# Masks and selector of a windowed attention built behind the branch instead of ahead of it (one Trainium2 core)

## The chip, the core and the metric

The kernel runs on one core of one Trainium2 chip. The metric is the device time of one execution in microseconds (us). Engines are named as in the profile: PE is TensorE, DVE is VectorE, ACT is ScalarE, POOL is GpSimd, SP is SyncE, which issues the transfers (DMAs). A "q" behind a name (DVEq) is the engine's sequencer, which runs register and branch instructions.

## The reference

Attention with a local window and a few global keys and a distance bias, then two gated convolution networks:

```python
scores = scale * np.matmul(q, k.transpose(0, 1, 3, 2))        # B, H, S, D = 2, 8, 768, 64
is_global = pos[None, :] < int(n_global)                      # 8
is_local = (rel >= 0) & (rel < int(n_local))                  # 96
dist = np.where(is_global & ~is_local, float(n_local), np.abs(rel))
scores = np.where(keep, scores + -slopes * dist, -1000000000.0)
a = softmax(scores)                                           # keep = is_global | is_local
x = np.matmul(a, v)                                           # to (B, S, 512)
x = (sigmoid(causal_conv5(x)) * (x @ w_val)) @ w_out
h = np.maximum(x @ w_in, 0.0)                                 # 1024 wide
out = (h * sigmoid(conv3(h))) @ w_out2
```

## The kernel before

**Tiles.** The attention runs over 12 tiles of 128 queries (2 sequences x 6). A tile sees its own 128 keys and the 128 before them (a window of 256 columns); the first tile of a sequence sees only its own. Into the first 32 columns of the block before, which no query of the window reaches, the first keys of the sequence are copied (`first_keys`), so that the global keys are in the window too.

**One tile.** `scores` makes the scores of four heads at a time on PE (L293); VectorE adds the bias and finds the extreme (L301 with the bias array `B` for a tile with two blocks; L303 to L305 with the distance array `d0` for a tile with one block); ACT takes the exponential (L307). `weights_t` transposes the result on PE (L350, against the identity `ident`) and ACT copies it back (L352); `outputs` multiplies with the values (L362). `sums`, `turn` and `spread` bring the reciprocal sums into the layout of the output with a small matmul against a constant, the selector `sel` (L340). Between these steps `fill()` takes the next piece of other work: weights come in 0.5 MB pieces (`fetch`, L108), are converted from the form in which they lie in memory (`to_f32`, L82 to L86) and prepared, and later the dense networks run.

**The constants.** `positions` makes the index arrays `rel`, `ge` and `key` from two iotas. `masks` makes from them and from the two limits (`lf`, from `li`, read from memory) the arrays `loc`, `d0`, `k0` and `d`, and from `d` the bias `B` of the eight heads, on GpSimd (L248). `selector` makes `sel` with a memset and two selects on GpSimd (L203, L206) and a copy on ACT (L210). All of these use parts of the tile `x` as scratch.

**The branch.** The kernel has two arms: a fast one for limits that fit the window, and a general one. Every engine loads the two limits from memory into registers (L704), compares them and branches (L754). An engine does this in its own order of instructions: behind whatever the program put ahead of it. `positions`, `masks`, `make_identity` and `selector` stand ahead of the branch; SP's transfers of the limits and of the first tile's keys and queries too (L699, L701). All other transfers are issued behind it.

**The order.** On PE the instructions stand as written. On the other engines a scheduler orders them by its own estimates; `first()` (L376 to L408) raises the first tiles' steps above the fills. `fast_attention` begins with transfers, then the first tile's scores, and then goes through the tiles `t`, with `START` = 6 of them in a loop of its own.

Of the kernel before, what the change touches and what calls it, by code (L numbers as in the profile page):

```python
# [12 lines left out]
AF = mybir.ActivationFunctionType  # L13
ALU = mybir.AluOpType
# [3 lines left out]
P = 128  # L18
# [8 lines left out]
WIN = 2 * P  # L27
# [8 lines left out]
BIG = NEG * 2.0 ** NH * 1.01  # L36
# [21 lines left out]
def slope(h):  # L58
    return 2.0 ** (-8.0 * (h + 1) / NH)
# [139 lines left out]
def selector(c):  # L199

    nc = c.nc
    e = c.x[0 : 2 * NH, 0:2, XP : XP + 2 * P].rearrange("r a (h d) -> r a h d", d=D)
    nc.gpsimd.memset(e, 1.0)  # L203

    for sign, base in ((1, 0), (-1, 1)):
        nc.gpsimd.affine_select(  # L206
            out=e, in_=e, compare_op=ALU.is_ge, fill=0.0, base=base, pattern=[[-8 * sign, 2], [-2 * sign, 4], [0, D]], channel_multiplier=sign
        )
    c.sel = c.const.tile([2 * NH, NPAIR, P], F32R, name="sel")
    nc.scalar.activation(c.sel.rearrange("r (a n) c -> r a (n c)", a=2), e.rearrange("r a h d -> r a (h d)"), AF.Copy)  # L210


def positions(c):

    nc = c.nc
    t = c.x[:, 2:4, XP : XP + 3 * WIN].rearrange("p a (n w) -> p a n w", w=WIN)
    c.rel, c.ge, c.loc = (t[:, 0, n] for n in range(3))
    c.key, c.k0, c.d = t[:, 1, 0, 0:P], t[:, 1, 0, P:], t[:, 1, 1]
    it, ic = t[:, 1, 1].bitcast(I32), t[:, 1, 2, 0:P].bitcast(I32)
    nc.gpsimd.iota(it, pattern=[[-1, WIN]], base=P, channel_multiplier=1)  # L220
    nc.vector.tensor_copy(c.rel, it)
    nc.vector.tensor_scalar(c.ge, c.rel, 0.0, None, ALU.is_ge)
    nc.gpsimd.iota(ic, pattern=[[1, P]], base=0, channel_multiplier=0)
    nc.vector.tensor_copy(c.key, ic)


def masks(c):


    nc = c.nc  # L230
    lf = c.const.tile([P, 2], F32, name="lf")
    nc.vector.tensor_copy(lf, c.li[:, :, 0])
    ng, nl = lf[:, 0:1], lf[:, 1:2]
    rel, loc, d, key, k0 = c.rel, c.loc, c.d, c.key, c.k0
    c.d0 = d0 = c.const.tile([P, P], F32, name="d0")
    nc.vector.scalar_tensor_tensor(loc, rel, nl, c.ge, ALU.is_lt, ALU.mult)
    nc.vector.scalar_tensor_tensor(d0, rel[:, P:], nl, loc[:, P:], ALU.subtract, ALU.mult)
    nc.vector.scalar_tensor_tensor(k0, key, ng, loc[:, P:], ALU.is_lt, ALU.max)
    nc.vector.tensor_scalar(k0, k0, -BIG, BIG, ALU.mult, ALU.add)
    nc.vector.scalar_tensor_tensor(d0, d0, nl, k0, ALU.add, ALU.add)  # L240
    nc.vector.tensor_scalar(key[:, 0:GW], key[:, 0:GW], ng, None, ALU.is_lt)
    nc.vector.tensor_scalar(d, loc, -BIG, BIG, ALU.mult, ALU.add)
    nc.vector.tensor_scalar(d[:, 0:GW], key[:, 0:GW], -BIG, BIG, ALU.mult, ALU.add)
    nc.vector.tensor_tensor(d[:, GW:], d[:, GW:], rel[:, GW:], ALU.add)
    nc.vector.tensor_scalar(d[:, 0:GW], d[:, 0:GW], nl, None, ALU.add)
    c.B = c.const.tile([P, NH, WIN], F32, name="B")
    for h in range(NH):
        nc.gpsimd.tensor_scalar(c.B[:, h, :], d, -slope(h) / QKSCALE, 1.0, ALU.mult, ALU.mult)  # L248


def fast_attention(c, ap, fill):
# [6 lines left out]
    nc, ident = c.nc, c.ident  # L258
# [4 lines left out]
    def load_kq(t):  # L263
        if t:
            kq[t] = ap.tile([P, NPAIR, 2, P], F32, tag="kq", bufs=KQBUFS, name="kq")
            nc.sync.dma_start(kq[t], c.kq[tiles[t]])
        else:
            kq[t] = c.first
# [75 lines left out]
    def weights_t(t, pr, tags="tx"):  # L344
        nw = len(blocks(t))
        pt = c.psum.tile([P, 2, 2, P], F32, tag=tags[pr % 2], name="pt")
        for z in range(2):
            w = p.pop((t, 2 * pr + z))
            for j in range(nw):
                nc.tensor.transpose(pt[:, z, j, :], w[:, j * P : (j + 1) * P], ident)  # L350
        pts[t, pr] = ap.tile([P, 2, 2, P], F32, tag="pts", bufs=PTBUFS, name="pts")
        nc.scalar.activation(pts[t, pr][:, :, :nw, :], pt[:, :, :nw, :], AF.Copy)  # L352
# [28 lines left out]

    load_kq(0)
    load_kq(1)
    fill()
    load_v(0)
    load_kq(2)
# [6 lines left out]
    for t in range(START):  # L393
        after = t + 1 < START
        if t:
            load_kq(t + 2)
        with first():
            weights_t(t, 0, "ff")
            if t:
                turn(t - 1)  # L400
            if after:
                scores(t + 1, 0)
            if t:
                spread(t - 1)
            weights_t(t, 1, "ff")
        for n in range(FILLS[t] // 2):
            fill()
        with first():  # L408
            weights_t(t, 2, "ff")
            if after:  # L410
                scores(t + 1, 1, "o")
                first_keys(t + 1)
            if t:
                scaled(t - 1)
            weights_t(t, 3, "ff")
            sums(t)
        for n in range(FILLS[t] // 2, FILLS[t]):
            fill()
        if after:
            with first():  # L420
                outputs(t)
            load_v(t + 2)
# [260 lines left out]
@with_exitstack  # L683
def attention_gated_mlps(ctx, tc, kq, v, nn, w_val, conv_w, w_out, w_in2, w_out2, out):
    nc = tc.nc
    c = Ctx()
    c.nc, c.tc, c.kq, c.v, c.out = nc, tc, kq, v, out
    c.nn = nn.bitcast(I32)
    c.w_val, c.conv_w, c.w_out, c.w_in2, c.w_out2 = (w.bitcast(I32) for w in (w_val, conv_w, w_out, w_in2, w_out2))

    c.const = ctx.enter_context(tc.tile_pool(name="const", bufs=1))
    c.big = ctx.enter_context(tc.tile_pool(name="big", bufs=BIGBUFS))
    c.wst = ctx.enter_context(tc.tile_pool(name="wst", bufs=1))
    c.sg = ctx.enter_context(tc.tile_pool(name="sg", bufs=1))
    c.x = new_x(c)

    c.first = c.x[:, 0:2, XP + 2 * P : XP + 6 * P].rearrange("p j (n t s) -> p j n t s", n=2, t=2)
    c.li = c.const.tile([P, 2, 2], I32, name="li")
    nc.sync.dma_start(c.li.rearrange("p n t -> p (n t)"), c.nn.to_broadcast([P, 4]))  # L699
    for j in range(2):  # L700
        nc.sync.dma_start(c.first[:, j], kq[0, 0, :, 2 * j : 2 * j + 2])  # L701
    positions(c)
    masks(c)
    _, (glo, ghi, llo, lhi) = nc.values_load_multi_w_load_instructions(c.nn)  # L704
    narrow = (llo >= 1) * (llo <= PREV + 1) * (glo >= 0) * (glo <= GW) * ((lhi | ghi) == 0)
    one = c.const.tile([P, 1], F32, name="one")
    nc.vector.memset(one, 0.0)
    nc.scalar.activation(one, one, AF.Exp)
    c.ident = c.const.tile([P, P], F32, name="ident")
    make_identity(nc, c.ident)  # L710
    selector(c)

    def psum_tiles(pool):
        bufs = {"s": 2, "t": 1, "x": 1, "f": 2, "o": 2}
        r = Ctx()
        r.tile = lambda shape, dt, tag, name: pool.tile(shape, dt, tag=tag, name=name, bufs=bufs[tag])
        return r

    chunks = [(b, ch) for b in range(NB) for ch in range(NCH)]

    def arm(fast):
        with ExitStack() as es:
            c.psum = psum_tiles(es.enter_context(tc.tile_pool(name="ps", bufs=1, space=PSUM)))
            c.inputs, c.written, c.taken, c.wo2 = [], 0, 0, []
            c.ready = inputs(c, chunks)

            def between():
                yield from weights(c)
                yield from dense(c, chunks)

            work = between()
            fills = iter(range(1 << 20))

            def fill():
                if next(fills) == 1:
                    load_conv_weights(c)
                next(work, None)

            with tc.tile_pool(name="at", bufs=1) as ap:
                if fast:  # L740
                    with tc.manual_schedule(engines={mybir.EngineType.PE}):
                        fast_attention(c, ap, fill)
                        for _ in work:
                            pass
                else:
                    load_conv_weights(c)
                    for b, _ in enumerate(full_attention(c, ap)):

                        while c.taken < (b + 1) * NCH:
                            next(work)  # L750
                    for _ in work:
                        pass

    with tc.If(narrow != 0) as cmp:  # L754
        arm(True)
    with cmp.Else():
        arm(False)
# [40 lines left out]
```

## Time and profile before

| | |
|---|---|
| median of 3 runs | 319.53 us (319.44 to 320.73) |
| profiled execution | 318.94 us, of which its span (first to last instruction) is 317.2 us |
| PE busy | 285.9 us, 90% of the span |
| DVE busy | 239.2 us, 75% |
| ACT busy | 208.4 us, 66% |
| POOL busy | 11.0 us, 3% |
| mean TensorE clock granted | 0.982 of 2.4 GHz |

Times in the profile count from the start of the span. Busy times leave out register, branch and transfer-issuing instructions. PE's matmuls are pipelined, so a busy PE is not PE at its peak.

### The profile page before, as it was taken

Reading aid. Unit: us, or ns where it says so; the run is one execution under the profiler, and the core shown is the slowest. Engines: PE = TensorE matmul, PEld = TensorE weight load, DVE = VectorE, ACT = ScalarE, POOL = GpSimd, SP = SyncE. Lnnn points to the kernel's source line nnn. Section 1 sums busy time; section 2 is a strip of 40 time slices with the busy share of each in tenths; the row PEclk is TensorE's granted clock in tenths of the full one; section 3 lists DMA queues with packets and bytes.
Section 4 is the critical chain, followed back from the end, with each engine's and each line's share of the span. In section 5 each row is a group of like instructions: output and inputs, shape, how many; then the busy total and the mean of one; then the engine's idle time right before and its main releaser. Section 6 shows DMA issues by size and latency. Waiting matters only on the chain.

```text
span 317.2 us, 5891 instructions
## 1 busy us (share of the span) xinstructions
PE 285.9 (90%) x2156; PEld 241.6 (76%) x2156; DVE 239.2 (75%) x660; ACT 208.4 (66%) x522; POOL 11.0 (3%) x31
## 2 busy tenths in 40 slices
PE   2169799797899999999999999999899989999993
PEld 2048556466867579999899988998899979999982
DVE  5397999989799998897765688673698379833750
ACT  2197897967596489688585786862577168615651
POOL 4400000200000000000000000000000000000000
PEclk9996999999799999999999999999999999999999
DMA  4993391257432302030210100100000001000002
GB/s 151 339 402 143 122 308 52 68 178 274 164 132 69 110 22 69 2 107 3 83 59 33 44 0 3 42 35 0 2 33 35 0 0 68 0 2 34 35 1 76
DMA packets 9494, 26.21 MB, mean 83 GB/s; under 512 B 1392, under 2 KB 1392, under 8 KB 9456
## 3 DMA queue, kind: packets, MB, share of 16 engines
q1 hardware_dynamic: 9456, 25.74, 23.0%
q8 instruction: 19, 0.31, 0.4%
q14 instruction: 19, 0.16, 0.1%
HBM read 22.59 MB, written 3.15 MB: 81 GB/s over the span
## 4 chain that ended last, share of the span: by engine, by line
PE 66%; DVE 16%; ACT 9%; DMA 5%; issue 2%; DVEq 1%; ACTq 0%; SPq 0%
PE po L74 7%; PE po L76 7%; PE ph L74 7%; PE ph L75 7%; PE po L75 7%; PE ph L76 6%; PE xp L362 5%; PE pt L350 4%; PE s L293 4%; PE pv L74 4%; PE pv L75 4%; PE pv L76 3%; ACT p L307 3%; DVE p L301 3%; DVE z L536 3%
## 5 line engine op out<-in xcount | busy, mean ns | idle before, releaser
L307 ACT ACTIVATE p<-p,st 128x256 f32<-128x256 f32 (+1 forms) x96 | 45.8, 479 | 18.3 <-DVE st L301 10.8
L74 PE MATMUL ph<-gg,Wh 128*128 128x258 f32 x192 | 55.9, 291 | 0.6 <-DVE Wl L69 0.6
L75 PE MATMUL ph<-gg,Wh 128*128 128x258 f32 x192 | 54.6, 284 | 1.6 <-DVE gg L69 1.6
L76 PE MATMUL ph<-gg,Wl 128*128 128x258 f32 x192 | 53.8, 280 | 0.0
L536 DVE SCALAR_TENSOR_TENSOR zh<-h,cw,zh 128x256 f32<-128x256 f32 x96 | 44.7, 481 | 11.0 <-ACT zh L534 9.2
L536 DVE SCALAR_TENSOR_TENSOR z<-x,cw,z 128x258 f32<-128x258 f32 x96 | 40.0, 480 | 1.7 <-ACT z L534 1.7
L350 PE MATMUL pt<-ident,p 128*128 128x128 f32 x176 | 27.6, 289 | 14.7 <-ACT p L307 10.0
L75 PEld LDWEIGHTS ph<-gg,Wh 128*128 128x128 f32 x192 | 36.4, 189 | 3.7 <-DVE gg L69 2.0
L74 PEld LDWEIGHTS ph<-gg,Wh 128*128 128x128 f32 x192 | 36.1, 188 | 3.1 <-DVE Wl L69 0.8
L74 PE MATMUL po<-wo,g 128*128 128x512 f32 x96 | 38.2, 398 | 0.0
L76 PE MATMUL po<-wo,g 128*128 128x512 f32 x96 | 37.9, 395 | 0.0
L75 PE MATMUL po<-wo,g 128*128 128x512 f32 x96 | 37.7, 393 | 0.0
L76 PEld LDWEIGHTS ph<-gg,Wl 128*128 128x128 f32 x192 | 36.6, 191 | 0.0
L350 PEld LDWEIGHTS pt<-ident,p 128*128 128x128 f32 x176 | 20.3, 145 | 20.5 <-issue 9.0
L301 DVE CUSTOM_DVE_ANT_0 p<-s,B 128x256 f32<-128x256 f32 x80 | 29.0, 418 | 2.1 <-PE s L293 2.0
L74 PE MATMUL pv<-gx,wvh 128*128 128x258 f32 x96 | 28.4, 295 | 0.8 <-DVE Wl L69 0.8
L352 ACT ACTIVATE pts<-pt 128x512 f32<-128x512 f32 (+1 forms) x48 | 24.9, 552 | 5.0 <-PE pt L350 4.9
L75 PE MATMUL pv<-gx,wvh 128*128 128x258 f32 x96 | 28.0, 291 | 0.0
L76 PE MATMUL pv<-gx,wvl 128*128 128x258 f32 x96 | 27.7, 289 | 0.0
L620 ACT ACTIVATE h<-ph 128x258 f32<-128x258 f32 x48 | 18.1, 378 | 12.2 <-PE ph L76 11.7
L293 PE MATMUL s<-kq 64*128 64x128 f32 x320 | 25.8, 296 | 0.0
L293 PEld LDWEIGHTS s<-kq 64*128 64x128 f32 x320 | 21.6, 198 | 5.0 <-issue 4.0
(99 smaller groups left out, 539.0 us busy)
## 6 DMA issues: line engine op xcount, KB each, us to landing
raw<-in_moe_w_out_dram SPq DMA_DIRECT2D x12, 512.0 KB, 4.0
kq<-in_kq_dram SPq DMA_DIRECT2D x11, 512.0 KB, 4.1
raw<-in_moe_w_in_dram SPq DMA_DIRECT2D x8, 512.0 KB, 5.5
v<-in_v_dram SPq DMA_DIRECT2D x12, 256.0 KB, 3.1
out_dram<-o SPq DMA_DIRECT2D x12, 256.0 KB, 2.0
raw<-in_moe_w_val_dram SPq DMA_DIRECT2D x4, 512.0 KB, 4.8
x<-in_kq_dram SPq DMA_DIRECT2D x2, 256.0 KB, 3.5
v<-in_v_dram SPq DMA_DIRECT2D x8, 64.0 KB, 2.5
```

Of the source, the lines that this page charges most:

```text
L74: nc.tensor.matmul(out, lh, rh, start=first, stop=False)
L75: nc.tensor.matmul(out, lh, rl, start=False, stop=False)
L76: nc.tensor.matmul(out, ll, rh, start=False, stop=last)
L293: nc.tensor.matmul(out, rows_of(t, pr, 1)[hs], rows_of(j, pr, 0)[hs], start=True, stop=True)
L301: nc.vector.tensor_tensor_reduce(w, sc, c.B[:, h, :], -QKSCALE, 3.0e38, ALU.add, ALU.min, mn)
L307: nc.scalar.activation(w[:, :nk], w[:, :nk], AF.Exp, bias=mn, scale=scale, accum_out=sm)
L350: nc.tensor.transpose(pt[:, z, j, :], w[:, j * P : (j + 1) * P], ident)
L352: nc.scalar.activation(pts[t, pr][:, :, :nw, :], pt[:, :, :nw, :], AF.Copy)
L362: nc.tensor.matmul(xp[z * D : (z + 1) * D, pr, :], vs[j][:, 2 * pr + z, :], w[:, z, n, :], start=n == 0, stop=n == len(js) - 1,)
L536: nc.vector.scalar_tensor_tensor(z, src[:, k : k + n], w[:, k : k + 1], z, ALU.mult, ALU.add)
L620: nc.scalar.activation(h[:, f % 2, :], ph[:, :HW], AF.Relu, scale=0.25)
```

## The change

`masks` is called inside the fast arm, behind the issue of the first transfers; `selector` inside the loop over the tiles, in the first pass. `positions` stays ahead of the branch, behind the identity. In `masks` the product `loc` is made in two halves of 128 columns, with `d0` and `k0`, which the first tile needs, between them in the source. The selector's copy goes from ACT to GpSimd.

```diff
@@ selector
-    nc.scalar.activation(c.sel.rearrange("r (a n) c -> r a (n c)", a=2), e.rearrange("r a h d -> r a (h d)"), AF.Copy)
+    nc.gpsimd.tensor_scalar(
+        c.sel.rearrange("r (a n) c -> r a (n c)", a=2), e.rearrange("r a h d -> r a (h d)"), 1.0, 1.0, ALU.mult, ALU.mult
+    )
@@ masks
-    nc.vector.scalar_tensor_tensor(loc, rel, nl, c.ge, ALU.is_lt, ALU.mult)
-    nc.vector.scalar_tensor_tensor(d0, rel[:, P:], nl, loc[:, P:], ALU.subtract, ALU.mult)
-    nc.vector.scalar_tensor_tensor(k0, key, ng, loc[:, P:], ALU.is_lt, ALU.max)
-    nc.vector.tensor_scalar(k0, k0, -BIG, BIG, ALU.mult, ALU.add)
-    nc.vector.scalar_tensor_tensor(d0, d0, nl, k0, ALU.add, ALU.add)
+    for z in (slice(P, WIN), slice(0, P)):
+        nc.vector.scalar_tensor_tensor(loc[:, z], rel[:, z], nl, c.ge[:, z], ALU.is_lt, ALU.mult)
+        if z.start:
+            nc.vector.scalar_tensor_tensor(d0, rel[:, z], nl, loc[:, z], ALU.subtract, ALU.mult)
+            nc.vector.scalar_tensor_tensor(k0, key, ng, loc[:, z], ALU.is_lt, ALU.max)
+            nc.vector.tensor_scalar(k0, k0, -BIG, BIG, ALU.mult, ALU.add)
+            nc.vector.scalar_tensor_tensor(d0, d0, nl, k0, ALU.add, ALU.add)
@@ fast_attention
     load_kq(1)
+    masks(c)
     fill()
...
             weights_t(t, 1, "ff")
+        if t == 0:
+            selector(c)
         for n in range(FILLS[t] // 2):
@@ attention_gated_mlps
-    positions(c)
-    masks(c)
     _, (glo, ghi, llo, lhi) = nc.values_load_multi_w_load_instructions(c.nn)
...
     make_identity(nc, c.ident)
-    selector(c)
+    positions(c)
```

Line numbers of the changed kernel are 2 to 7 higher than those of the kernel before from `masks` on.

VectorE, from the end of its work ahead of the branch to the first tile's first score operation (`x` holds the scratch arrays, `d_81` is `d0`, `p` the scores with bias). Before:

```order
L240 SCALAR_TENSOR_TENSOR d_81<-d_81,lf,x 128x128
L243 TENSOR_SCALAR x<-x 128x32
L244 TENSOR_TENSOR x<-x 128x224
L245 TENSOR_SCALAR x<-x,lf 128x32
L704 TENSOR_LOAD in_n_dram_ptr
L704 TENSOR_LOAD in_n_dram
L754 COMPARE_AND_BRANCH
L303 SCALAR_TENSOR_TENSOR p<-d_81,s_266 128x128
```

And with the change (L239 to L249 are `masks`, L307 the first score operation, L308 the reduce behind it):

```order
L223 CAST x<-x 128x256
L226 CAST x<-x 128x128
L224 TENSOR_SCALAR x<-x 128x256
L709 TENSOR_LOAD in_n_dram_ptr
L709 TENSOR_LOAD in_n_dram
L759 COMPARE_AND_BRANCH
L234 CAST lf<-li 128x2
L239 SCALAR_TENSOR_TENSOR x<-x,lf 128x128 x2
L248 TENSOR_TENSOR x<-x 128x224
L307 SCALAR_TENSOR_TENSOR p<-d_214,s_262 128x128
L249 TENSOR_SCALAR x<-x,lf 128x32
L83 TENSOR_SCALAR raw<-raw 128x512 x2
```

The register loads now stand ahead of the masks. The scheduler put both halves of L239 side by side and all of `masks` but its last instruction (L249, before: L245) ahead of the first score operation; L249 stands behind the first tile's last reduce, and two conversions of weights (L83) follow.

GpSimd, from the iotas to the bias arrays. Before:

```order
L223 IOTA x 128x128
masks.py:197 MEMSET ident 128x128
L203 MEMSET x 16x2x256
masks.py:199 AFFINE_SELECT ident<-ident 128x128
L206 AFFINE_SELECT x<-x 16x2x256 x2
L248 TENSOR_SCALAR B<-x 128x256 x8
L704 TENSOR_LOAD in_n_dram_ptr
L704 TENSOR_LOAD in_n_dram
L754 COMPARE_AND_BRANCH
L313 TENSOR_SCALAR gl<-x 128x128
```

And with the change:

```order
L225 IOTA x 128x128
L709 TENSOR_LOAD in_n_dram_ptr
L709 TENSOR_LOAD in_n_dram
L759 COMPARE_AND_BRANCH
L317 TENSOR_SCALAR gl<-x 128x128
L203 MEMSET x 16x2x256
L206 AFFINE_SELECT x<-x 16x2x256 x2
L210 TENSOR_SCALAR sel<-x 16x512
L252 TENSOR_SCALAR B<-x 128x256 x8
```

The selector's four instructions and the eight of `B` moved behind the branch, and the copy of the first keys (`gl`) ahead of them.

ACT, in the first and the second tile (128x128 is an exponential of the first tile, 128x256 of the second, `ina` converted weights). Before:

```order
L307 ACTIVATE p,st<-p,st 128x128 x4
L82 ACTIVATE ina<-raw 128x512
L307 ACTIVATE p,st<-p,st 128x256 x4
L352 ACTIVATE pts<-pt 128x2x128 x2
L307 ACTIVATE p,st<-p,st 128x256 x4
L307 ACTIVATE p,st<-p,st 128x128
```

And with the change:

```order
L311 ACTIVATE p,st<-p,st 128x128 x5
L356 ACTIVATE pts<-pt 128x2x128
L311 ACTIVATE p,st<-p,st 128x256 x2
L356 ACTIVATE pts<-pt 128x2x128
L311 ACTIVATE p,st<-p,st 128x256 x6
```

The first tile's last exponential moved ahead of the second tile's, and the conversion of weights (L82) behind them.

## Rows read from the trace of the kernel before

**Rows 1.** Busy time in two stretches: start and end, length, each engine (instructions), granted clock.

```profile
14.76:90.00 75.24, 64.43 (x501) 47.16 (x502) 69.59 (x222) 60.98 (x170) 3.49 (x6) 0.93 0.54 193
90.00:200.00 110.00, 109.23 (x904) 93.22 (x903) 91.97 (x270) 81.60 (x219) 1.23 (x4) 1.00 0.15 49
```

**Rows 2.** The chain that ended last, its first long piece: start, length, what.

```profile
0.80 3.08 DMA li<-in_n_dram
```

**Rows 3.** Line 704, the register loads: duration in ns (least/median/most), start in us.

```profile
L704 PEldq TENSOR_LOAD <-in_n_dram_ptr x1: 908/908/908, 0.9 to 0.9; - x1
L704 PEldq TENSOR_LOAD <-in_n_dram x1: 1697/1697/1697, 1.9 to 1.9; - x1
L704 SPq TENSOR_LOAD <-in_n_dram_ptr x1: 1342/1342/1342, 2.2 to 2.2; - x1
L704 SPq TENSOR_LOAD <-in_n_dram x1: 592/592/592, 3.6 to 3.6; - x1
...
L704 DVEq TENSOR_LOAD <-in_n_dram_ptr x1: 2468/2468/2468, 7.6 to 7.6; - x1
...
L704 DVEq TENSOR_LOAD <-in_n_dram x1: 2232/2232/2232, 10.1 to 10.1; - x1
```

**Rows 4.** Timeline, DVE and PE, 4 to 14 us: start, busy, what [idle before].

```profile
4.64 0.49 DVE L236 SCALAR_TENSOR_TENSOR x<-x,lf 128x256 f32<-128x256 f32 x1
...
4.94 2.08 PE L293 MATMUL s<-x 64*128 64x128 f32 x16 [4.94 <-DMA x<-in_kq_dram]
...
5.51 0.74 DVE L238 SCALAR_TENSOR_TENSOR x<-x,lf 128x128 f32<-128x128 f32 x1
...
7.11 0.34 DVE L240 SCALAR_TENSOR_TENSOR d<-d,lf,x 128x128 f32<-128x128 f32 x1
...
7.76 0.23 DVE L245 TENSOR_SCALAR x<-x,lf 128x32 f32<-128x32 f32 x1
...
13.17 0.29 DVE L303 SCALAR_TENSOR_TENSOR p<-d,s 128x128 f32<-128x128 f32 x1 [5.18 <-issue]
```

**Rows 5.** Timeline, POOL, 5 to 21 us.

```profile
5.16 0.28 POOL masks.py:199 TENSOR_SCALAR_AFFINE_SELECT ident<-ident 128x128 f32<-128x128 f32 x1
5.40 1.56 POOL L206 TENSOR_SCALAR_AFFINE_SELECT x<-x 16x512 f32<-16x512 f32 x2
8.08 3.33 POOL L248 TENSOR_SCALAR B<-x 128x256 f32<-128x256 f32 x8 [1.11 <-DVE x L245]
...
20.25 0.30 POOL L317 TENSOR_SCALAR kq<-gl 128x128 f32<-128x128 f32 x1 [5.08 <-issue]
```

**Rows 6.** Timeline, DVE and ACT, 16 to 23 us.

```profile
16.65 0.42 DVE L83 TENSOR_SCALAR raw<-raw 128x512 int32<-128x512 int32 x1
...
17.18 0.68 DVE L84 SCALAR_TENSOR_TENSOR raw<-raw 128x512 int32<-128x512 int32 x1
...
17.90 0.42 DVE L301 CUSTOM_DVE_ANT_0 p<-s,B 128x256 f32<-128x256 f32 x1
...
20.28 0.42 DVE L301 CUSTOM_DVE_ANT_0 p<-s,B 128x256 f32<-128x256 f32 x1
...
22.85 0.39 ACT L307 ACTIVATE p<-p,st 128x128 f32<-128x128 f32 x1
```

**Rows 7.** A transfer's issue (timeline, SP), and its kind: KB each, median us to landing, before 24 us.

```profile
7.79 0.37 SPq L266 DMA_DIRECT2D kq<-in_kq_dram  x1
...
kq<-in_kq_dram SPq DMA_DIRECT2D x3, 512.0 KB, 8.5
```

**Rows 8.** Busy time and granted clock from 20 to 28 us (columns as in rows 1); timeline, PE.

```profile
20.00:24.00 4.00, 1.02 (x6) 0.54 (x6) 4.00 (x19) 4.00 (x16) 0.30 (x1) 0.82 0.94 375
24.00:28.00 4.00, 4.00 (x31) 3.25 (x31) 3.38 (x13) 2.70 (x7) 0.00 (x0) 0.50 0.52 177
...
26.95 2.08 PE L293 MATMUL s<-kq 64*128 64x128 f32 x16
...
30.76 1.16 PE L293 MATMUL s<-kq 64*128 64x128 f32 x16
```

## Prediction

> **What bounds the kernel now.** I began with the page's busy times: PE works 90% of the span (the table above), so TensorE sets the end wherever it has work to do. The windows say where it has: from 90 to 200 us PE is busy 109.2 of 110.0 us, from 14.76 to 90 us 64.4 of 75.2 us [rows 1], and before 14.76 us hardly at all. What is saved there must come from the stretch before 14.76 us, and it reaches the end only if all that follows can begin earlier too.
>
> So I read the chain of waits from its beginning. Its first piece is the transfer of the two limits, 0.80 to 3.88 us [rows 2], which is what VectorE waits for before the masks. Then come VectorE's mask instructions, to 7.99 us (L245), and then nothing until 13.17 us: 5.18 us that the timeline calls issue, that is, without a wait for another engine or a transfer [rows 4]. The rows of line 704 tell what this is: every engine reads the two limits into registers for the branch, with two loads in a row, and VectorE's loads took 2.47 and 2.23 us, starting at 7.6 and 10.1 us [rows 3]. The first score operation of the first tile (L303) starts at 13.17 us [rows 4], 0.85 us after the second load's end (10.1 + 2.23 = 12.3). PE had made those scores by 7.02 us [rows 4] and stood idle. The same two loads took PE 0.91 + 1.70 = 2.61 us at the start, and SP 1.34 + 0.59 = 1.93 us from 2.2 us on [rows 3]. What differs is the hour: when its own loads are done, at 4.2 us (3.6 + 0.59), SP goes on to issue all the large transfers. Their effect on the loads is my reading of these rows, not a row of its own.
>
> **The change, step by step.**
>
> *VectorE reaches the branch earlier.* Ahead of it there stay two casts and a comparison, which need only GpSimd's two iotas; the identity's memset and select (0.28 us [rows 5]) now stand before or between these. SP begins its loads at 2.2 us; I take 2.1 us for VectorE. The limits' transfer no longer holds it there: it has landed (3.88 us) when the masks come.
>
> *The loads.* I take PE's pair, 2.61 us, because it too ran beside another engine's loads; now four engines load between 2 and 5 us. That gives 4.7 us, and with the same 0.85 us behind it the first mask instruction at 5.55 us. The ends: SP's pair, 1.93 us (0.7 earlier), and VectorE's own, 4.70 us (2.1 later). The Trainium skill (DMA: Bandwidth & Descriptors, "Latency and other measured facts") gives about 600 ns as the floor of such a load; the trace agrees in SP's second (0.59 us) and in no other; two at that floor would make the gain about 1.4 us larger.
>
> *The masks ahead of the first score.* Now they run from 4.64 us (L236) to 7.76 us (start of L245): 3.12 us [rows 4]. L245's counterpart stands behind the first tile now. Added are the cast of the limits (at most L245's 0.23 us) and the split of L236 into two halves of 128 columns (twice L240's 0.34 less 0.49: 0.2 us). So 3.5 us, and the first score at 9.05 instead of 13.17 us: **4.1 us earlier**. PE's scores are ready by then, and their keys come with transfers that don't move.
>
> How far GpSimd stretches this is the doubtful part. Today L238 took 0.74 us beside the selector's two selects (1.56 us), where L240, of the same kind and shape, took 0.34 us with GpSimd idle [rows 4, 5]. In the changed kernel the same selects, the copy of the first keys (0.30) and the selector's copy (512 columns on 16 partitions; 0.30 us at 128 and 3.33/8 = 0.42 us at 256 columns make some 0.65 us, an estimate) fall into the same stretch, so I leave today's stretching in. Without any, two such delays (L238 and L239) go: 0.7 us earlier. With every one of these 0.30 + 1.56 + 0.65 = 2.5 us added to an unstretched 2.8 us, the first score is at 10.85 us, 1.8 us later.
>
> ACT loses the selector's copy, which lay in ACT's wait for the first exponential: nothing. GpSimd's copy is needed only by the spreading matmuls behind the third tile's first scores, which start at 26.95 us [rows 8]: nothing beyond the stretching above. That lines P to WIN of the masks are made first by itself gains nothing I can price: the order below puts nearly all of the masks ahead of the first score all the same.
>
> *The eight biases B.* Today they run from 8.08 to 11.41 us [rows 5], while VectorE stands still. Now they wait for L245's counterpart, behind the eighth head of the first tile, and take 3.33 us beside a busy VectorE. They are due one by one: the next tile's first score operation (L301) came 4.73 us after the first L303 (17.90 - 13.17), and its second four 7.11 us after it (20.28 - 13.17) [rows 6]. The first tile's own share of the 4.73 us is 3.6 us (less an L83 and an L84), so B starts near 12.7 us. Up to the second four the new order adds L245 (0.23) and one L83 (0.42) and drops an L86 (as long as an L84, 0.68) and an L83 for an L84 and a small sum (some 0.2): net +0.4 us, so 16.55 instead of 20.28 us. The two L83 and two L84 on this way can each wait for a B: between nothing and 4 x 0.42 = 1.7 us. L301 itself doesn't seem to: GpSimd's copy at 20.25 us lay beside an L301 that took 0.42 us, its usual time [rows 5, 6]. I take the middle, 0.85 us: **0.4 + 0.85 us given back**, 2.9 us left. By the Trainium skill (SBUF — State Buffer, "Who interferes with whom") a VectorE instruction in a two-port mode or with two SBUF inputs and a GpSimd instruction that reads SBUF exclude each other, whichever starts first; one with a single SBUF input is free. On L301 the trace agrees; taken at its word for the rest it gives the second rival.
>
> *ACT's order.* Today the last exponential of the first tile stands behind all of the next tile's (22.85 us, 0.39 us [rows 6]) and the transposes wait for it. Now it stands ahead: **0.4 us won**, 3.3 us in all.
>
> *What carries it to the end.* PE's order is unchanged instruction for instruction. VectorE and ScalarE are reordered as far as about 100 us, but do the same work there, and from 14.76 to 90 us VectorE is busy 69.6 of 75.2 us and ScalarE 61.0 [rows 1]: all of it follows the first score, so it slides as one. The first transfers don't slide, since SP's way to them is unchanged. The 0.5 MB keys of the third tile are issued at 7.79 us and land, by the median of their kind, 8.5 us later [rows 7], near 16.5 us; PE uses them at 26.95 us now and would at 23.6: still in time. The later weight transfers wait for buffers and slide with the work.
>
> The sum: 4.1 - 0.4 - 0.85 + 0.4 = 3.3 us. The profiled execution took 318.94 us, 0.6 us under the median of 319.53 us; from the median that makes **316.2 us**. No change means within 0.5%, 1.6 us, about what a measurement of this kernel tells apart.
>
> **Rivals.**
>
> *More than that.* The loads take SP's 1.93 us (+0.7), nothing is stretched (+0.7) and B excludes nobody (+0.85): 5.5 us, 314.0 us. For it: L301 beside GpSimd kept its time. Against: L238 did not. The granted clock could add to it: 0.50 (1.2 GHz) from 24 to 28 us, after four microseconds in which PE was busy 1.02 us, made 16 score matmuls take 2.08 us where they took 1.16 us at 2.4 GHz [rows 8]. If that low stretch falls on other work the time moves by a microsecond either way. Chance 0.18.
>
> *Given back on the port.* GpSimd and VectorE exclude each other for every shared microsecond: the first score at 10.85 us (-1.8) and B's full 1.7 us (another -0.85): 0.65 us left, 318.9 us, no change. Also here: the gain is swallowed because a reordered conversion of weights comes too late for a matmul. Chance 0.16 together.
>
> *The loads block each other (slower).* PE's second load took 1.70 us while SP's first was under way; SP's second, beside nobody, 0.59 us [rows 3]. If each further engine adds such 1.1 us, four sharers make 0.59 + 4.4 = 5.0 us a load and 10 us a pair instead of 2.6: VectorE's first score comes later than today, and SP's first large transfer too: 3.3 - 7.4 = 4.1 us lost, 323.6 us. It decides from a pair of 5.9 us on. Against it: SP's first load was beside PE's second and took only 1.34 us. Chance 0.06.
>
> **How the numbers follow.** The forecast, 316.2 with 314.7 to 317.8 of its own for the bounds of load and port that don't fall together, has 0.60. Faster by over 0.5% (below 317.9) is the forecast and the first rival, 0.78; no change 0.16; slower 0.06. The range leaves out the slow rival, half of the unchanged cases and a little of the best: 313.8 to 318.4.
>
> **What would show it.** Right: VectorE's pair of loads from about 2.1 us and no longer than 2.6 us; first mask instruction near 5.6 us, first score near 9 us (8.3 to 10.9), the next tile's second four near 17.4 us, its last exponential near 20 us, and from there every stage about 3.3 us earlier. The loads are wrong if the pair takes over 4 us; the port is wrong if L238's and L239's counterparts are short, or if L83 and L84 beside B are as short as today; the carrying is wrong if the first score is early and the stage at 90 us is not. A first score later than 12 us would refute the forecast.

## The result, and the profile after

The changed kernel took **315.59 us** (median of 20 runs, 314.26 to 318.56), the kernel before 319.44 us beside it (20 runs, 317.32 to 324.29). The ratio is 0.9906, with a 95% interval of 0.9882 to 0.9930: 2.2 to 3.8 us faster, 3.0 us in the middle. The ratio is taken over the fast runs alone, so it is not the quotient of the two medians, and it is the one to go by. The forecast was 316.2 us, 3.3 us faster; its range of 313.8 to 318.4 us holds the time. The profiled execution took 314.69 us, with a span of 313.0 us where the kernel before had 317.2.

Busy times on the page of the changed kernel:

```profile
span 313.0 us, 5893 instructions
PE 283.6 (91%) x2156; PEld 239.8 (77%) x2156; DVE 240.4 (77%) x661; ACT 208.1 (66%) x521; POOL 12.0 (4%) x32
```

The work is the same but for one VectorE instruction more, one on ScalarE less and one on GpSimd more. The two stretches of [rows 1], in the changed kernel:

```profile
14.76:90.00 75.24, 62.97 (x528) 45.39 (x526) 70.81 (x216) 62.11 (x167) 4.48 (x11) 0.98 0.56 201
90.00:200.00 110.00, 108.98 (x885) 94.10 (x886) 89.95 (x263) 81.47 (x218) 1.24 (x4) 1.00 0.14 47
```

Before 90 us PE is busy 62.97 us instead of 64.43, with 27 more matmuls in the stretch and a granted clock of 0.98 instead of 0.93, and behind 90 us it is as busy as it was (108.98 and 109.23 us): the work slid forward, and PE still waits before 90 us. The loads of the two limits, now line 709 (columns as in [rows 3]):

```profile
L709 PEldq TENSOR_LOAD <-in_n_dram x1: 1647/1647/1647, 1.9 to 1.9; - x1
L709 DVEq TENSOR_LOAD <-in_n_dram_ptr x1: 1504/1504/1504, 2.0 to 2.0; - x1
...
L709 DVEq TENSOR_LOAD <-in_n_dram x1: 591/591/591, 3.6 to 3.6; - x1
```

VectorE's pair takes 1.50 + 0.59 = 2.10 us where it took 4.70 us [rows 3]. Its timeline (columns as in [rows 4]; L307 and L305 are L303 and L301 of before). Scores come in groups of four heads; the "second four" is the second group of the second tile, here the line at 16.60 us:

```profile
5.01 0.17 DVE L234 CAST lf<-li 128x2 f32<-128x2 int32 x1 [2.55 <-issue]
...
6.52 0.68 DVE L243 TENSOR_SCALAR x<-x 128x128 f32<-128x128 f32 x1
...
8.01 0.80 DVE L248 TENSOR_TENSOR x<-x 128x224 f32<-128x224 f32 x1
8.73 0.47 DVE L307 SCALAR_TENSOR_TENSOR p<-d,s 128x128 f32<-128x128 f32 x2
...
12.49 0.75 DVE L83 TENSOR_SCALAR raw<-raw 128x512 int32<-128x512 int32 x2
13.16 0.68 DVE L84 SCALAR_TENSOR_TENSOR raw<-raw 128x512 int32<-128x512 int32 x1
14.14 0.42 DVE L305 CUSTOM_DVE_ANT_0 p<-s,B 128x256 f32<-128x256 f32 x1 [0.30 <-POOL B L252]
...
16.00 0.69 DVE L84 SCALAR_TENSOR_TENSOR raw<-raw 128x512 int32<-128x512 int32 x1
16.60 0.41 DVE L305 CUSTOM_DVE_ANT_0 p<-s,B 128x256 f32<-128x256 f32 x1
```

The first score operation starts at 8.73 us instead of 13.17 [rows 4], 4.44 us earlier. The second tile's second four start at 16.60 instead of 20.28 us [rows 6], 3.68 us earlier: 0.76 us were given back on the way. `B` has 0.30 us of this by the wait shown, and some 0.2 us more: the first four L305 of the second tile start at 14.14, 14.62, 14.99 and 15.38 us, 1.24 us from first to last, where the second four take 1.03 us. GpSimd's timeline, and the instructions that write `B` (the columns of [rows 3]):

```profile
12.60 4.83 POOL L252 TENSOR_SCALAR B<-x 128x256 f32<-128x256 f32 x8 [4.03 <-DVE st L309]
```

```profile
L252 POOL TENSOR_SCALAR B<-x x8: 404/405/1512, 12.6 to 17.0; 128x256 f32<-128x256 f32 x8
```

The one of them that starts at 16.1 us, by itself:

```profile
L252 POOL TENSOR_SCALAR B<-x x1: 798/798/798, 16.1 to 16.1; 128x256 f32<-128x256 f32 x1
```

`B` takes 4.83 us instead of 3.33 [rows 5]. Two of the eight are longer than the 0.40 us of the other six. The first took 1.51 us: it lies beside two L83 and an L84. The seventh took 0.80 us: it lies beside the L84 at 16.00 us. The VectorE instructions kept their 0.42 us (L83) and 0.68 us (L84; the two L83 take 0.75 us together, as they overlap).

How far the gain reaches is seen from SyncE's first transfers of results, first before and then after the change:

```profile
164.54 2.51 SPq L637 DMA_DIRECT2D out_dram<-o  x2
```

```profile
159.68 2.50 SPq L644 DMA_DIRECT2D out_dram<-o  x2
```

Here the distance is 4.9 us, over 1 us more than at 16.6 us. The two executions differ in their granted clock as well: that of before was at 0.52 of full speed from 22.80 to 29.60 us and at 0.53 from 80.80 to 84.20 us, that of after at 0.55 from 49.10 to 52.50 us (and both in about their last microsecond). The interval from the many runs, 2.2 to 3.8 us, is what counts for the change. The clock is not what makes it: over their runs the mean granted clock was 0.984 for the changed kernel and 0.981 for the kernel before (its 85 runs beside the experiments). A difference of 0.003 over 316 us is 1.9 us at half speed, where PE's work takes 1.8 times as long [rows 8]: at most 0.9 of the 3.0 us, an estimate.

### The profile page after: what moved, and what is told of

It reads as the page before. It is cut to its first block, busy times and chain, and to the rows that moved or that the text cites. A ratio compares the mean times of both kernels' runs of the same rounds, so it can differ in the third digit from the quotient of the medians.

```text
span 313.0 us, 5893 instructions
## 1 busy us (share of the span) xinstructions
PE 283.6 (91%) x2156; PEld 239.8 (77%) x2156; DVE 240.4 (77%) x661; ACT 208.1 (66%) x521; POOL 12.0 (4%) x32
## 4 chain that ended last, share of the span: by engine, by line
PE 66%; DVE 17%; DMA 7%; ACT 5%; issue 2%; POOL 1%; DVEq 0%; POOLq 0%; ACTq 0%; SPq 0%
PE ph L74 7%; PE ph L75 7%; PE ph L76 7%; PE po L74 7%; PE po L76 7%; PE po L75 7%; DMA raw<-in_moe_w_out_dram 5%; PE xp L366 4%; PE s L297 4%; PE pv L74 3%; PE pv L75 3%; PE pv L76 3%; PE pt L354 3%; DVE p L305 3%; PE wps L178 2%
## 5 line engine op out<-in xcount | busy, mean ns | idle before, releaser
L305 DVE CUSTOM_DVE_ANT_0 p<-s,B 128x256 f32<-128x256 f32 x80 | 29.1, 418 | 0.7 <-PE s L297 0.4
L74 PE MATMUL pv<-gx,wvh 128*128 128x258 f32 x96 | 27.8, 290 | 0.3 <-DVE Wl L69 0.3
L75 PE MATMUL pv<-gx,wvh 128*128 128x258 f32 x96 | 27.3, 284 | 0.0
L366 PE MATMUL xp<-pts,v 128*64 128x128 f32 x352 | 22.5, 277 | 4.3 <-ACT pts L356 3.5
```

The lines of the kernel that those rows point to most:

```text
L74: nc.tensor.matmul(out, lh, rh, start=first, stop=False)
L75: nc.tensor.matmul(out, lh, rl, start=False, stop=False)
L305: nc.vector.tensor_tensor_reduce(w, sc, c.B[:, h, :], -QKSCALE, 3.0e38, ALU.add, ALU.min, mn)
L366: nc.tensor.matmul(xp[z * D : (z + 1) * D, pr, :], vs[j][:, 2 * pr + z, :], w[:, z, n, :], start=n == 0, stop=n == len(js) - 1,)
```

## The experiments

**What the masks give, and what the selector gives.** The theory: the masks' new place is the gain, because VectorE loads the limits before the large transfers are on their way; the selector's move and the split into halves give nothing. The rival: the selector's move, which takes a copy from ScalarE and work from in front of the branch, has a good share.

The masks alone behind the branch:

```diff
     positions(c)
-    masks(c)
...
     load_kq(1)
+    masks(c)
     fill()
```

> Only the masks move behind the branch; the selector, its copy on ACT and the undivided loc stay as before. Theory (VectorE's two register loads leave the stretch of the large transfers): VectorE's pair takes about 2.1 us from 2.0 us on as in the changed kernel, the first mask instruction starts near 5 us, the first score operation between 8 and 9.3 us (13.17 before, 8.73 changed), and the time is within 1 us of the changed kernel's, 2 to 4 us under before. GpSimd reaches the branch late, since the selector's memset waits for the keys (4.7 us): its pair takes 3 us or more, and B is made after it, still before 18 us. Rival (the selector's move carries a good part): less than half the gain, under 1.5 us.

Measured: 316.39 us, ratio 0.9918 (0.9886 to 0.9949). The first score operation started at 8.15 us, the second four at 16.65 us. That is nearly the whole gain, 2.6 of 3.0 us by the ratios.

The selector alone behind the branch, with its copy on GpSimd:

```diff
-    nc.scalar.activation(c.sel.rearrange("r (a n) c -> r a (n c)", a=2), e.rearrange("r a h d -> r a (h d)"), AF.Copy)
+    nc.gpsimd.tensor_scalar(
...
-    selector(c)
...
             weights_t(t, 1, "ff")
+        if t == 0:
+            selector(c)
```

> Only the selector moves behind the branch, with its copy on GpSimd; the masks stay ahead. Theory: VectorE's loads still start behind the masks, at about 7 us or later, in the stretch of the large transfers, and take 4 us or more; the first score operation comes at 12.3 to 13.2 us (0.7 us at most from masks that no select stretches), time within 1 us of before. Rival (the selector's move carries a good part): the first score or the second tile's scores more than 1.5 us earlier and the time 1.5 us or more under before.

Measured: 317.52 us, ratio 0.9975 (0.9947 to 1.0002), not told apart from no change. The first score came at 11.45 us, earlier than I expected: without the selects beside them the masks were done sooner, and the loads, from 6.5 us, took 2.55 + 1.56 us instead of 2.47 + 2.23 us.

The changed kernel without the halves, `loc` made in one instruction of 256 columns:

```diff
-    for z in (slice(P, WIN), slice(0, P)):
-        nc.vector.scalar_tensor_tensor(loc[:, z], rel[:, z], nl, c.ge[:, z], ALU.is_lt, ALU.mult)
...
+    nc.vector.scalar_tensor_tensor(loc, rel, nl, c.ge, ALU.is_lt, ALU.mult)
```

> The changed kernel with loc made in one instruction of 256 columns, as before. Theory: the scheduler puts the masks ahead of the first score operation all the same, so the halves gain nothing: first score operation 0.1 to 0.4 us earlier than 8.73 us, time within 0.7 us of the changed kernel. Rival (the first half first is what lets the first tile begin): first score operation later than 9 us and a time over 1 us above the changed kernel.

Measured: 316.28 us, ratio 0.9911 (0.9878 to 0.9944), the first score at 8.27 us. The halves cost 0.46 us at the front, and nothing that shows in the time.

**Are the loads slow because of the transfers?** The kernel before, where SyncE first issues a transfer of 16 bytes that waits for the masks, so that it reaches the branch, and with it the large transfers, late:

```diff
     masks(c)
+    nc.sync.dma_start(c.rel[:, P : P + 4].bitcast(I32), c.nn.to_broadcast([P, 4]))
     _, (glo, ghi, llo, lhi) = nc.values_load_multi_w_load_instructions(c.nn)
```

> The kernel before, with one small transfer more on SP ahead of its branch (16 bytes a partition into scratch that the masks have just read), so that SP waits for the end of the masks and issues the large transfers about 3.5 us later. Everything on VectorE stays. Theory (the large transfers make the register loads slow): VectorE's loads still start at 7.6 us, but the pair takes 2.0 to 2.8 us instead of 4.7, and the first score operation comes at 10.5 to 11.4 us instead of 13.17, although nothing was moved on VectorE. Rival (loads behind a compute engine's work are slow by themselves, or the engines' loads hinder each other): the pair still takes 4 us or more, first score at 12.7 us or later.

Measured, in a single run: 319.15 us. Its loads, SyncE's first large transfer, and VectorE's first weight step:

```profile
L705 DVEq TENSOR_LOAD <-in_n_dram_ptr x1: 908/908/908, 7.4 to 7.4; - x1
...
L705 DVEq TENSOR_LOAD <-in_n_dram x1: 1509/1509/1509, 8.4 to 8.4; - x1
```

```profile
10.71 0.33 SPq L266 DMA_DIRECT2D kq<-in_kq_dram  x1
```

```profile
15.81 0.43 DVE L83 TENSOR_SCALAR raw<-raw 128x512 int32<-128x512 int32 x1 [1.52 <-DMA raw<-in_moe_w_in_dram]
```

VectorE's loads, at about the hour of before (7.4 instead of 7.6 us) but ahead of the large transfers, take 2.42 instead of 4.70 us. So the transfers do slow them. Holding the transfers back is no way to use that: the first score was at 10.72 us, 2.45 us early, but VectorE then waited 1.52 us for its first weight transfer, the second four started at 19.64 us, and the run took as long as the kernel before.

**Is it the start, or the new order behind the branch?** The change also makes the scheduler order VectorE's and ScalarE's work differently, by the traces up to about 132 us, and I had only argued that this gives nothing. So the start had to move with the old order. First try, the register loads in a critical section ahead of the casts:

```diff
     for j in range(2):
         nc.sync.dma_start(c.first[:, j], kq[0, 0, :, 2 * j : 2 * j + 2])
+    with tc.tile_critical():
+        _, (glo, ghi, llo, lhi) = nc.values_load_multi_w_load_instructions(c.nn)
...
     positions(c)
     masks(c)
-    _, (glo, ghi, llo, lhi) = nc.values_load_multi_w_load_instructions(c.nn)
```

> The kernel before with the two register loads of every engine in a critical section ahead of the casts and masks; every instruction of VectorE, ScalarE, TensorE and GpSimd otherwise stands where it stood before, so nothing behind the branch is reordered. Theory (the earlier start is the gain): VectorE's pair of loads takes 1.7 to 2.6 us from about 2 us, the first score operation starts between 7.6 and 9.2 us instead of 13.17, the second four of the next tile near 16 us instead of 20.28, and the time is 2.5 to 4 us under that of before. Rival (the gain of the change came from the reordering of VectorE and ScalarE behind the branch, the early start being lost again): the first score is as early, but the time is less than 1 us under that of before. A second rival: the critical section holds SyncE back until its first transfers have landed, the large transfers start more than 1 us later than at 4.2 us, and that takes part of the gain back.

Measured: 318.39 us, ratio 0.9972 (0.9942 to 1.0002). The second rival came true: all engines waited until the first keys had landed, loaded together from 5.6 us, and the first large transfer went out at 8.41 us. The first score was at 12.05 us, only 1.1 us early, so this run doesn't answer the question. Second try, the same section ahead of the transfers of the first keys:

```diff
+    with tc.tile_critical():
+        _, (glo, ghi, llo, lhi) = nc.values_load_multi_w_load_instructions(c.nn)
...
     c.x = new_x(c)
...
     masks(c)
-    _, (glo, ghi, llo, lhi) = nc.values_load_multi_w_load_instructions(c.nn)
```

> As the kernel before, with the register loads of every engine moved to the very top, ahead of the casts, the masks and SyncE's transfers of the first keys; behind the branch every engine keeps the order of the kernel before. Theory (the earlier start is the gain): SyncE's first large transfer goes out within 1.5 us of before's 4.2 us, VectorE's first score operation starts between 8 and 10 us instead of 13.17, the second four of the next tile between 16 and 17.5 us instead of 20.28, and the time is 2.3 to 4 us under that of before. Rival (the reordering behind the branch gave the gain of the changed kernel): the first score is as early, and the time is less than 1 us under that of before. Between the two, both have a share.

Measured: **316.34 us, ratio 0.9909 (0.9870 to 0.9948)**. VectorE's loads and its timeline in this kernel:

```profile
L696 DVEq TENSOR_LOAD <-in_n_dram_ptr x1: 972/972/972, 3.7 to 3.7; - x1
...
L696 DVEq TENSOR_LOAD <-in_n_dram x1: 545/545/545, 4.7 to 4.7; - x1
```

```profile
9.56 0.29 DVE L303 SCALAR_TENSOR_TENSOR p<-d,s 128x128 f32<-128x128 f32 x1 [0.83 <-PE s L293]
...
17.23 0.41 DVE L301 CUSTOM_DVE_ANT_0 p<-s,B 128x256 f32<-128x256 f32 x1
```

Every engine keeps the order of before, masks and selector stay ahead of the branch, and the time is that of the changed kernel. The first score is 3.6 us early, the second four 3.05 us, the time by the ratio 2.9 us. The transfers went out later than I expected (7.21 us, 2.3 us after before's 4.92 us), and no wait for them shows in this stretch; the first score waits 0.83 us for PE's scores, since the first keys, too, are transferred only behind the loads (issued at 5.39 us, in the changed kernel at 1.24). The theory stands: the early start makes the gain, and the changed kernel's own order adds nothing that can be measured.

**Does GpSimd's stretching cost time?** The changed kernel once more, and beside it the changed kernel with the selector's scratch over the masks' scratch, which makes GpSimd build the selector after `B`:

```diff
-    e = c.x[0 : 2 * NH, 0:2, XP : XP + 2 * P].rearrange("r a (h d) -> r a h d", d=D)
+    e = c.x[0 : 2 * NH, 2:4, XP + WIN : XP + 2 * WIN].rearrange("r a (h d) -> r a h d", d=D)
```

> The changed kernel again, beside the next three on the same chip: 2 to 4 us under before.

> The changed kernel with the selector's scratch laid over two arrays of the masks (ge and d), so that its four instructions on GpSimd come behind B instead of beside the masks. Theory (GpSimd's selects and copy stretch the masks, L243, L244 and L248 by some 0.35 us each): the masks take 2.6 to 3.0 us instead of 3.7, the first score operation starts at 7.7 to 8.1 us instead of 8.73, and the time falls by 0.3 to 1.2 us. Rival (those three instructions are as long for another reason): first score within 0.2 us of 8.73, same time.

Measured: 315.30 us, ratio 0.9888 (0.9843 to 0.9933), for the changed kernel; 315.74 us, ratio 0.9912 (0.9880 to 0.9944), with the selector later. VectorE's masks in the latter:

```profile
6.50 0.21 DVE L243 TENSOR_SCALAR x<-x 128x128 f32<-128x128 f32 x1
6.78 0.34 DVE L244 SCALAR_TENSOR_TENSOR d<-d,lf,x 128x128 f32<-128x128 f32 x1
7.13 0.38 DVE L248 TENSOR_TENSOR x<-x 128x224 f32<-128x224 f32 x1
```

The stretching is real: 0.21 us instead of 0.68, 0.38 instead of 0.80, and the first score at 7.43 us. But the time didn't follow. Soon after, an L83 waits 0.40 us for a weight transfer that goes out when it always did, and the 1.16 us that are left at the second four (15.44 us) aren't found in the time: its ratio is no lower than that of the changed kernel (0.9906 and 0.9888). The two intervals leave room for a gain of about a microsecond, and where the lead goes is not shown.

**All of the masks first.** In the changed kernel, L249, which finishes `d`, stands behind the first tile's scores, and `B` waits for it. With the masks raised as a whole it stands ahead:

```diff
     load_kq(1)
-    masks(c)
+    with first():
+        masks(c)
```

> The changed kernel with all of masks in the raised priority, so that its last instruction (L249) stands ahead of the first tile's scores and B can start before them. Theory (B beside the conversions of weights costs only what its port takes: its waits of 0.30 and 0.2 us): B starts near 9 us and is done by 13.5 us, the two L83 and the L84 are no longer stretched, the second tile's first L305 starts at 13.5 to 13.9 us instead of 14.14, and the time falls by 0 to 0.7 us. Rival (B beside a busy VectorE is a large cost of this change): over 1 us less.

Measured: **310.63 us, ratio 0.9742 (0.9701 to 0.9783)**, 4.7 us below the changed kernel beside it. I had expected at most 0.7 us. `B` now runs from 9.00 to 12.35 us and is as short as before (3.35 us). With the selector's move of above added:

> The last two together: selector behind B, masks raised. Theory: first score at 7.8 to 8.3 us, second tile's first L305 at 12.6 to 13.2 us instead of 14.14, time 0.5 to 1.7 us under the changed kernel, if all of it carries; less if the transfers set the pace by then (the third and fourth pieces of weights land near 13 and 15 us). Rival: no difference from the changed kernel beyond 0.3 us.

Measured: 310.86 us, ratio 0.9765 (0.9726 to 0.9804): once more nothing for the selector.

The 4.7 us can't come from the first microseconds: the second four start at 16.47 us here and at 16.60 us in the changed kernel. Nor is it the clock: the run with the selector added had a mean of 0.985, the changed kernel beside it 0.989. But the edit also changed the scheduler's order of VectorE and ScalarE (not of PE and GpSimd), by the traces up to about 143 us. Two runs tell the early `B` and the order apart. In the first, every engine keeps the order of all masks first, but GpSimd writes each `B` twice:

```diff
-    for h in range(NH):
+    for h in [*range(NH), *range(NH)]:
         nc.gpsimd.tensor_scalar(c.B[:, h, :], d, -slope(h) / QKSCALE, 1.0, ALU.mult, ALU.mult)
```

> The kernel with all masks first, with the eight biases B written twice over by GpSimd, so that the valid ones are done about as late as in the changed kernel (near 16 to 17.5 us instead of 12.35); the order on the four other engines is that of the kernel with all masks first. Theory A (the further gain of 4.7 us came from the different order of VectorE's and ScalarE's work behind the second tile): the time stays within 1 us of 310.6 us. Theory B (it came from B being ready early and unstretched): the time goes back to between 313.5 and 316 us.

Its GpSimd row:

```profile
8.99 7.94 POOL L252 TENSOR_SCALAR B<-x 128x256 f32<-128x256 f32 x16 [0.48 <-DVE x L249]
```

Measured: 312.38 us (309.75 to 315.32), ratio 0.9776 (0.9720 to 0.9833). `B` is done at 16.93 us, about as late as in the changed kernel (17.43), and the second tile's two groups of four start at 14.05 and 16.39 us (changed kernel: 14.14 and 16.60). Most of the gain stays: by the ratios it is 1.1 us above all masks first (0.9742) and 3.6 us below the changed kernel (0.9888). Theory A's number, within 1 us of 310.6, was missed by the median, which lies 1.8 us above; theory B's band begins 1.1 us above that median. The intervals of all masks first and of this run overlap, so whether the late `B` costs a microsecond is not settled. In the second run the order is kept as well, but the start is as late as before: VectorE first copies a column of the first keys, so it must wait for them.

```diff
     positions(c)
+    nc.vector.tensor_copy(c.loc[:, 0:1], c.first[:, 1, 0, 0, 0:1])
```

> The kernel with all masks first, every engine in its order, with one added instruction: VectorE copies a column of the first keys ahead of its casts, so it reaches the register loads only when these keys have landed, and loads beside the large transfers as the kernel before does. VectorE's loads should start between 5.3 and 6.2 us and take 2.4 to 4.7 us together, and the first score operation start between 11.5 and 14 us (kernel before: 13.17; all masks first: 8.84). Theory (the early start and the order behind the branch are two gains that add): the start's delay of 2.7 to 5.2 us shows in the time nearly whole, 313 to 316 us, which is still 3 to 6 us under the kernel before although the first score is no more than 1.7 us earlier than there. Rival (that order is only better because the start is early): 317 us or more. A third way: the order takes the delay up, and the time stays within 1 us of 310.6 us.

Its loads (line 710) and its timeline:

```profile
L710 DVEq TENSOR_LOAD <-in_n_dram_ptr x1: 2547/2547/2547, 5.6 to 5.6; - x1
L710 DVEq TENSOR_LOAD <-in_n_dram x1: 1280/1280/1280, 8.2 to 8.2; - x1
```

```profile
12.88 0.48 DVE L307 SCALAR_TENSOR_TENSOR p<-d,s 128x128 f32<-128x128 f32 x2
...
20.51 0.42 DVE L305 CUSTOM_DVE_ANT_0 p<-s,B 128x256 f32<-128x256 f32 x1 [0.62 <-PE s L297]
```

Measured: 314.26 us, ratio 0.9817 (0.9772 to 0.9861). The first score is 0.3 us earlier than before the change and the second four 0.2 us later, and yet the time is 4.4 to 7.3 us shorter. The order alone does that. The start is a gain beside it: 4.0 us later at the first score make 3.6 us by the medians (314.26 against 310.63) and 2.4 us by the ratios, which allow for the two having run at different times beside other runs of the kernel before.

**Where the order of the changed kernel may lose.** ScalarE and VectorE in the changed kernel, at 42 us:

```profile
41.78 0.69 ACT L82 ACTIVATE inb<-raw 128x512 f32<-128x512 f32 x1 [1.77 <-DMA raw<-in_moe_w_in_dram]
```

```profile
44.47 0.17 DVE L326 TENSOR_SCALAR st<-st 128x8 f32<-128x8 f32 x1 [1.95 <-ACT p L311]
```

A weight conversion (L82) stands in ScalarE's queue and waits 1.77 us for its transfer; four exponentials that were ready to go stand behind it, and VectorE waits 1.95 us for the last of these. This wait is in all five traces with the changed kernel's order of ScalarE at this place (the changed kernel's two, masks alone, no halves, selector later; VectorE's part is 0.34 to 1.95 us), and in none of the four with all masks first. It isn't in the run with the loads at the top either, whose order is that of before and whose time is that of the changed kernel, so its absence alone makes no kernel fast. Later the chain that ended last goes through four weight transfers in the changed kernel:

```profile
61.83 4.61 DMA raw<-in_moe_w_in_dram
...
69.76 4.92 DMA raw<-in_moe_w_out_dram
...
77.90 3.42 DMA raw<-in_moe_w_out_dram
...
82.40 3.58 DMA raw<-in_moe_w_out_dram
```

With all masks first, the chain from 30 to 95 us holds one:

```profile
71.09 4.92 DMA raw<-in_moe_w_out_dram
```

The number alone decides nothing: the run with the loads at the top has two in this stretch of its chain, masks alone and no halves three. The last four pieces of w_out are issued from 71.09 us on there and from 74.51 us on in the changed kernel. The wait at 42 us could explain 0.3 to 2 of the 4.7 us; that the order makes the 4.7 us is shown, which of its moved steps do is not.

## Why the prediction was right, step by step

*The loads.* Priced at PE's pair, 2.61 us; VectorE's took 2.10 us, and the first mask instruction came at 5.01 us, where the forecast had 5.55. The rival that the loads block each other is refuted: five engines loading between 0.9 and 4.2 us took no pair above 2.6 us, and with nothing large under way five engines loaded at once in about 1.5 us each (the run with the loads at the top). My reading that the transfers slow the loads held in the run with SyncE late.

*The masks ahead of the first score.* Priced at 3.5 us, measured 3.72 us (5.01 to 8.73 us). Leaving today's stretching in was right: L243, L244 and L248 took two to three times what they take beside an idle GpSimd.

*The biases.* Here the sum was off, in the safe direction. I gave 0.4 us for the new order and 0.85 us for collisions with L83 and L84, 1.25 us between first score and second four; it was 0.76 us, some 0.5 us of it waits for `B` and some 0.25 us the new order. By its own sign ("if L83 and L84 beside B are as short as today") the forecast had the port wrong, that is, who pays: the collision is there, but GpSimd paid it (1.51 us for the first `B`, 0.80 us for the seventh) while L83 and L84 kept their times; VectorE paid when it came for those `B` that were late. The Trainium skill (SBUF — State Buffer, "Who interferes with whom") says that a VectorE instruction in a two-port mode or with two SBUF inputs and a GpSimd instruction that reads SBUF exclude each other, whichever starts first, and that a VectorE instruction outside such a mode with a single SBUF input is free. The trace agrees as far as it goes: the `B` that started inside an L83 and the one that started inside an L84 waited, the six beside L305 and other work took 0.40 us. No row here shows what L83 is to that rule. The rival "given back on the port" took the rule at its word with VectorE as the one that pays; it fell because in this place VectorE comes first. With the selector later GpSimd came first, and there VectorE did pay: an L83 of 0.63 us and an L84 of 0.87 us beside `B`.

*ACT's order and the carrying.* The second tile's last exponential starts at 18.60 us:

```profile
18.60 0.49 ACT L311 ACTIVATE p<-p,st 128x256 f32<-128x256 f32 x1
```

In the kernel before, the last one of this stretch started at 22.85 us [rows 6]. That is 4.25 us earlier, 0.57 us more than at the second four, where I had priced the new order of ScalarE at 0.4 us. So the front's lead is 4.25 us where the sum had 3.3, and from there I let everything slide as one. In the two profiled executions it did (4.9 us at the first results, 4.25 us in their times), but that pair has a clock of 0.993 against 0.982. Over all runs the gain is 3.0 us, so about one microsecond of the front's lead does not reach the end. With the order of before (the loads at the top) a lead of 3.05 us at the second four made 2.9 us by the ratio; with the changed order, leads of 3.63, 3.68 and 4.84 us (masks alone, the changed kernel, selector later) made 2.6, 3.0 and 2.8 us. That would fit an order that loses a little, but the intervals are too wide to show it. That 3.3 and 3.0 us lie so close is in part luck: the front gave more than forecast, and less of it was carried. That the reordering behind the branch "does the same work there" and slides as one was argued from busy times, and it reaches to 132 us, not 100. For this change it came out so, as the run with the old order shows. As a rule it was wrong: another order of the same work was worth 4.7 us. Busy times can't tell that, since what counts is which instruction stands at the head of a queue and waits.

*The rivals.* More than forecast (314.0 us): of its three parts, the loads brought 0.5 of 0.7 us, the way from the first score to the second four 0.5 us where 0.85 us were put down to `B`, and the stretching stayed. The slow one didn't come.

## What to carry to other kernels

On these runs a register load was cheap before the large transfers started and dear beside them: put the loads ahead of the work, and let the work follow the branch. When a scheduler orders the queues, every edit at the front is two edits, and the second can be the larger: compare the orders, and run the edit once with the old order and once with the new one started late. In a queue that runs in order, look for a conversion that waits for a transfer with ready work behind it that another engine needs.

## What the runs showed of the hardware that I had not expected

- The same pair of register loads on VectorE took 1.5 us with no large transfer under way (0.97 + 0.55), 2.1 us at 2 us beside the first keys, 2.4 us with the large transfers held back (why not 1.5 us there is not shown), and 3.8 to 4.7 us beside them (2.55 + 1.28, 2.55 + 1.56 and 2.47 + 2.23 us). The shortest second load of a pair took 0.50 us.
- GpSimd and VectorE slow each other in either direction: VectorE's 0.21, 0.34 and 0.38 us became 0.68, 0.74 and 0.80 us beside GpSimd's selects and copy, and GpSimd's 0.40 us became 1.51 us beside two L83 and an L84, and 0.80 us beside an L84, that kept their time. In these pairs the one that started second was the one stretched.
- One VectorE instruction of 0.23 us, moved from behind the first tile's scores to ahead of them, came with another order of the queues and 4.7 us of 315. The fastest kernel of this study, 310.63 us, is the changed kernel with its masks raised as a whole.
